# Hash attention and a SwiGLU layer in one kernel: earlier loads, and unit 1's x turned by DMA instead of TensorE

## The chip, the cores and the metric

The kernel runs on one core of a Trainium2 chip. The metric is the device time of one execution in microseconds (us). It is given as the median of several runs of the same program; 327.43 us is the median of three for the kernel before (327.17 to 328.53).

A core has five engines that run their own instruction streams: TensorE (PE, matmuls, with weight loads PEld beside them), VectorE (DVE), ScalarE (ACT), GpSimd (POOL) and SyncE (SP). SP computes nothing here; it issues DMAs, one after the other in the order written, and where a DMA must wait for something, all DMAs behind it on SP wait too. Sixteen DMA engines carry the data.

## The reference

```python
# attention: 4 batches, 8 heads, 768 rows, head size 64
q_bits = einsum('bhsd,dk->bhsk', q, proj) > 0        # 6 bits for each row; the same for k
mask   = bucket(q_bits)[..., :, None] == bucket(k_bits)[..., None, :]
scores = where(mask, q @ k.T / 8, -1e9)
attn   = exp(scores - max) / (sum + 1e-9)
x      = (attn @ v), heads side by side              # 3072 rows of 512
# feed-forward: 512 -> 1536 -> 512
xn  = x / sqrt(mean(x*x) + 1e-6) * rms_g
g   = xn @ w_gate
out = (g * sigmoid(g) * (xn @ w_val)) @ w_out
```

## The kernel before

The work is cut into eight **units**: unit u is half of batch u // 2, that is 384 query rows. In a unit there are eight heads, and a head is three **slots** of 256 keys each, so that attention is 192 slots, counted from 0. Heads of a batch go in four **pairs**; the text writes (1, 2) for batch 1, pair 2 (pairs count from 0, so it is the third pair of that batch). A pair's data are needed first by the unit of the batch's first half: pair (1, 2) by slot 60, in unit 2.

In slot t TensorE first computes the scores of slot t + 1 (`scores`, L345), ScalarE takes the exponential of slot t (`probs`, L357), and then whatever stands in `plan[t]` is recorded, in the order in which it was put there by `at(0, t, ...)`. There is no scheduler: each engine does its part of this list in that order, and waits where a semaphore tells it to. So the slot numbers in the code set the order on every engine, SP's DMA queue included, though not the time at which a DMA is issued: SP may run ahead of or behind the slots.

What the change touches, step by step:

- **Loads of a pair.** `load_natural` (L97) and `load_v` (L106) load q, k and v of a pair, 384 KB each, in three DMAs. From pair (1, 2) on `load_blocks` (L120) loads q and k instead in eight DMAs of 96 KB whose rows are 32 numbers (128 bytes) long. All go to a ring of eight buffers (`lpool`); a load waits until the last reader of its buffer is done.
- **Bits.** A pair's rows are multiplied by the projection on PE (`hash_pairs` L236 or `hash_one` L216), VectorE reads the signs (L225), and small DMAs carry these rows of bits into QK, the operand of the scores (`send_pair` L275, `send_bits` L304). A head's scores wait for its bits. `SENDS` gives the slot of such a send where it isn't that of the hash.
- **The turning of q and k** is done by PE for the pairs up to (1, 1) (L156) and by VectorE from (1, 2) on (`turn_dve`, L188 and L195); GpSimd then casts them into QK (`cast_pool`, L208).
- **v.** `v_prep` (L313) and `v_sum` (L319 to L321) are four GpSimd instructions for each pair. `zero_rows` (L146) is a GpSimd memset of one of six QK buffers.
- **x.** When a unit's heads are done, `norm` (L448, L456) scales its x, three thirds of 128 rows, and each third has to be turned, so that its 512 columns lie on the partitions. `turn_x` does that with four PE transposes into PSUM (L463) and one DVE multiplication by the column of weights `gcol` on the way out (L469, or L467 on ScalarE). `turn_dma` (L427) does it with one DMA transpose on SP's queue; the weights must then have been multiplied in before, along the row, and `norm` does that with `grow` (L448), a 128-row copy of `rms_g` that a DMA spreads and ScalarE multiplies by sqrt(512). `ONDMA` says how many of a unit's thirds go by DMA: two of three in units 2 to 6, one in unit 7, none in units 0 and 1.
- **The feed-forward part.** `gate` and `value` (L480) need all three thirds of the turned x (`xnT`). `project` (L509) and `store` (L521, L522) finish the unit before. `spread` places these pieces over the slots of the next unit: for unit 1 over slots 48 to 71. `norm(1)` stands in slot 52.
- **Weights.** Six `load_w` DMAs on GpSimd's queue (L581), 768 KB each, at slots 22 to 42, in the order wg, wv, wg, wv, wo, wo.

The table that places the pairs from (1, 2) on holds for each the slot of its loads, those of the turning of k and q, and that of the hash.

Of the kernel before, what the change touches and what calls it, by code (L numbers as in the profile page):

```python
# [19 lines left out]
DMODEL = H * D  # L20
# [13 lines left out]
def kernel(  # L34
# [12 lines left out]
    nc = tc.nc  # L47
# [27 lines left out]
    grow = const.tile([128, DMODEL], FP32, name="grow")  # L75
# [343 lines left out]

    rstds = {}  # L420

    ONDMA = {2: 2, 3: 2, 4: 2, 5: 2, 6: 2, 7: 1}

    def turn_dma(u, c):
        if c == 0:
# [16 lines left out]
    def norm(u):  # L442
# [3 lines left out]
        for c in range(3 if 0 < u < 7 else 2):  # L446
            if c < ONDMA.get(u, 0):
                nc.vector.scalar_tensor_tensor(  # L448
# [145 lines left out]
    def at(w, s, f, *a):  # L594
        plan[NS * w + s].append(lambda: f(*a))
# [70 lines left out]
    at(0, 1, load_natural, nc.sync, 0, 3, "q")  # L666
    at(0, 2, load_v, nc.sync, 0, 2)
    at(0, 2, load_v, nc.sync, 0, 3)
    at(0, 60, nc.sync.dma_start, grow, moe_rms_g.partition_broadcast(128))
    at(0, 65, nc.scalar.mul, grow, grow, float(DMODEL) ** 0.5)  # L670
    at(0, 6, v_prep, 0, 1)
    at(0, 15, v_prep, 0, 2)
    at(0, 19, v_prep, 0, 3, nc.vector)
# [6 lines left out]
        at(0, 39 + 3 * i, load_w, wo, moe_w_out, 6 * i, 6)  # L680


    for hp, ts in ((0, (8, 22, 23, 24, 25, 24, 39, 26, 28, 42)), (1, (20, 27, 28, 29, 30, 29, 41, 32, 33, 43))):
        tl, ts = ts[0], ts[1:]
        for w in "kq":
            at(0, tl, load_natural, nc.sync, 1, hp, w)
        at(0, tl, load_v, nc.sync, 1, hp)
        at(0, ts[0], new_pair, 1, hp)
        for t, hh, w in zip(ts[0:4], (0, 1, 0, 1), "kkqq"):
            at(0, t, turn_pe, 1, hp, hh, w)  # L690
        at(0, ts[4], cast_pool, 1, hp, "k")
        at(0, ts[5], cast_pool, 1, hp, "q")
        if hp == 0:
            at(0, ts[6], hash_pair, 1, hp)
            at(0, ts[7], send_pair, 1, hp)
        at(0, ts[8], v_prep, 1, hp)
        at(0, ts[8], v_sum, 1, hp)

    spots = {
# [10 lines left out]
    }  # L710
    for i, t in ((0, 39), (1, 41), (2, 57), (3, 61)):
        at(0, t, zero_rows, i)
    TX = 37

# [16 lines left out]
    for n, (u, h) in enumerate(order):  # L731
        t = 3 * n + 4 - ((u, h) == (0, H - 1))
# [46 lines left out]
            inserts[2 * b * NS + s] = (MEAN, v_mean, b, hp, 4)  # L779


    SENDS = {(2, 0, 0): 77, (2, 0, 1): 77, (2, 2, 1): 101, (3, 2, 1): 149}

    def place(t, step):
        at(0, t, *step)
        if step[0] is hash_one:
            late.append((t, hash_bits, *step[1:]))
            for hh in range(2):
                s = SENDS.get((*step[1:], hh), t)
                late.append((max(s, t), send_bits, *step[1:], hh))  # L790
# [26 lines left out]
    for u in range(7):  # L817
# [9 lines left out]
        at(0, t0 + 4, norm, u)  # L827
        for c in range(ONDMA.get(u, 0)):
            at(0, t0 + 5, turn_dma, u, c)
        pieces = []  # L830
        for i in range(9):
# [5 lines left out]
            if i in (6, 7):  # L837
                thirds = ((0,), (1, 2))[i - 6]
                for c in thirds:
                    if c >= ONDMA.get(u, 0):  # L840
                        pieces.append((TURN, False, [(0, turn_x, u, c)]))
# [10 lines left out]
    def behind_norm(t):  # L852

        return t - t % NS + 9 if 1 <= t % NS < 9 else t

    for (b, hp), (load, kturns, qturns, _) in spots.items():
        at(0, load, load_blocks, nc.sync, b, hp)
        at(0, load, load_v, nc.sync, b, hp)
        at(0, min(kturns + qturns), new_pair, b, hp)
        for w, turns in (("k", kturns), ("q", qturns)):  # L860
            for i, t in enumerate(turns):
                at(0, t, turn_dve, b, hp, w, i, len(turns))
            t = turns[-1] + 1
            at(0, t if (b, hp) == (1, 2) else behind_norm(t), cast_pool, b, hp, w)
        t = 54 if (b, hp) == (1, 2) else behind_norm(qturns[-1] + 2)
        at(0, t, v_prep, b, hp)
        at(0, t, v_sum, b, hp)

# [66 lines left out]
```

## Time and profile before

| | |
|---|---|
| median of three runs | 327.43 us (327.17 to 328.53) |
| the profiled execution | 327.66 us |
| its span, first to last instruction | 325.9 us (1.8 us lie around it) |
| PE busy | 321.1 us, 99% of the span |
| DVE, ACT, POOL busy | 231.0, 228.6, 157.6 us |
| granted TensorE clock | full in all 40 slices |
| moved by DMA | 32.6 MB, 100 GB/s on average, in 85,741 packets |

Times in the text are us from the span's start. "Busy" of PE is modelled: matmuls are pipelined, and what counts is the distance from the start of one to the start of the next. A row of the timeline gives the start, the length, engine, line, operation, tiles and the number of instructions merged into it; its length includes the latency of the last one.

By the starts of its scores on PE, slot 24 begins at 29.8 us, slot 48 at 62.8, slot 60 at 83.0 and slot 66 at 92.5.

### The profile page before, as it was taken

Reading aid. Unit: us, or ns where it says so; the run is one execution under the profiler, and the core shown is the slowest. Engines: PE = TensorE matmul, PEld = TensorE weight load, DVE = VectorE, ACT = ScalarE, POOL = GpSimd, SP = SyncE. Lnnn points to the kernel's source line nnn. Section 1 sums busy time; section 2 is a strip of 40 time slices with the busy share of each in tenths; the row PEclk is TensorE's granted clock in tenths of the full one; section 3 lists DMA queues with packets and bytes.
Section 4 is the critical chain, followed back from the end, with each engine's and each line's share of the span. In section 5 each row is a group of like instructions: output and inputs, shape, how many; then the busy total and the mean of one; then the engine's idle time right before and its main releaser. Section 6 shows DMA issues by size and latency. Waiting matters only on the chain.

```text
span 325.9 us, 7789 instructions
## 1 busy us (share of the span) xinstructions
PE 321.1 (99%) x2954; PEld 194.6 (60%) x2955; DVE 231.0 (71%) x514; ACT 228.6 (70%) x333; POOL 157.6 (48%) x204
## 2 busy tenths in 40 slices
PE   9999999999999999999999999999999999999996
PEld 4576666656566565655566556655656556665554
DVE  5887876869878659875888558886677536673870
ACT  6999887666688667777767668776777768754322
POOL 3999749955974353732783522753592111221000
PEclk9999999999999999999999999999999999999999
DMA  7942999989328828253547047002200030003002
GB/s 227 348 159 65 229 216 208 178 120 183 115 41 157 158 61 170 49 105 99 82 107 145 7 139 138 7 1 58 80 4 3 1 99 32 2 2 101 14 2 97
DMA packets 85741, 32.63 MB, mean 100 GB/s; under 512 B 70908, under 2 KB 82632, under 8 KB 85704
## 3 DMA queue, kind: packets, MB, share of 16 engines
q1 hardware_dynamic: 81800, 27.35, 35.9%
q0 software_dynamic: 3680, 4.72, 8.7%
q8 instruction: 23, 0.38, 0.5%
q14 instruction: 14, 0.11, 0.1%
q10 hardware_dynamic: 224, 0.07, 0.1%
HBM read 28.58 MB, written 6.29 MB: 107 GB/s over the span
## 4 chain that ended last, share of the span: by engine, by line
PE 98%; ACT 1%; issue 0%
PE s_ps L345 20%; PE g_ps L480 19%; PE v_ps L480 19%; PE y_ps L509 18%; PE o_ps L370 11%; PE d_ps L216 2%; PE t_ps L156 2%; PE d_ps L236 2%; PE z_ps L576 1%; PE x_ps L463 1%; PE y_ps L528 1%; PE m_ps L329 1%; ACT psb L357 1%; PE s_ps L156 0%; ACT ypart L533 0%
## 5 line engine op out<-in xcount | busy, mean ns | idle before, releaser
L357 ACT ACTIVATE psb<-s_ps,ebias 128x768 f16<-128x768 f32 x192 | 167.9, 900 | 21.3 <-PE s_ps L345 20.4
L345 PE MATMUL s_ps<-QK 128*128 128x384 f16 (+1 forms) x384 | 93.5, 326 | 1.2 <-ACT psb L357 1.1
L488 ACT ACTIVATE t<-g_ps 128x384 f32<-128x384 f32 x96 | 47.2, 492 | 51.1 <-PE g_ps L480 49.4
L480 PE MATMUL g_ps<-xnT,wg 128*128 128x384 f16 x384 | 82.7, 326 | 0.0
L480 PE MATMUL v_ps<-xnT,wv 128*128 128x384 f16 x384 | 81.8, 326 | 0.0
L497 DVE SCALAR_TENSOR_TENSOR a<-t,g_ps 128x384 f32<-128x384 f32 x96 | 52.9, 551 | 27.1 <-ACT t L488 25.4
L391 POOL TENSOR_TENSOR x<-otmp,rcp 128x384 f32<-128x384 f32 x30 | 25.1, 838 | 97.1 <-DVE rcp L389 96.9
L509 PE MATMUL y_ps<-wo,ht 128*128 128x512 f16 x276 | 67.7, 379 | 0.0
L498 DVE SCALAR_TENSOR_TENSOR ht<-a,v_ps 128x384 f16<-128x384 f32 x96 | 53.2, 554 | 12.0 <-PE v_ps L480 4.1
L370 PEld LDWEIGHTS <-psb 128*128 128x128 f16 x1152 | 51.9, 97 | 15.7 <-issue 1.2
L370 PE MATMUL o_ps<-vl,psb 128*128 128x65 f16 x1152 | 55.8, 193 | 0.0
L345 PEld LDWEIGHTS <-QK 128*128 128x128 f16 (+1 forms) x384 | 34.7, 98 | 34.9 <-issue 9.2
L480 PEld LDWEIGHTS <-wg 128*128 128x128 f16 x384 | 35.2, 97 | 21.2
L480 PEld LDWEIGHTS <-wv 128*128 128x128 f16 x384 | 35.1, 97 | 20.8 <-issue 0.2
L509 PEld LDWEIGHTS <-ht 128*128 128x128 f16 x276 | 24.9, 98 | 23.0
L521 ACT COPY ysb<-y_ps 128x512 f32<-128x512 f32 x23 | 13.5, 587 | 16.0 <-PE y_ps L509 16.0
L384 DVE TENSOR_TENSOR otmp<-o_ps,cvb 128x390 f32<-128x390 f32 x32 | 17.8, 558 | 7.2 <-PE o_ps L370 7.2
L208 POOL CAST QK<-qT 64x768 f16<-64x768 f32 x20 | 16.5, 823 | 10.4 <-DVE qT L195 9.5
L397 POOL TENSOR_TENSOR sq<-x 128x384 f32<-128x384 f32 x24 | 19.9, 827 | 1.9
L208 POOL CAST QK<-kT 64x768 f16<-64x768 f32 x20 | 16.4, 822 | 4.7 <-DVE kT L195 2.7
L469 DVE TENSOR_TENSOR xnT<-x_ps,gcol 128x512 f16<-128x512 f16 x11 | 7.4, 688 | 15.0 <-PE x_ps L463 14.9
L195 DVE STREAM_TRANSPOSE kT<-kL 128x192 f32<-128x192 f32 x32 | 16.4, 518 | 0.0
(85 smaller groups left out, 277.3 us busy)
## 6 DMA issues: line engine op xcount, KB each, us to landing
vn<-in_v_dram SPq DMA_DIRECT2D x16, 384.0 KB
out_dram<-ysb SPq DMA_DIRECT2D x23, 256.0 KB
qL<-in_q_dram SPq DMA_DIRECT2D x40, 96.0 KB
kL<-in_k_dram SPq DMA_DIRECT2D x40, 96.0 KB
kn<-in_k_dram SPq DMA_DIRECT2D x5, 384.0 KB
qn<-in_q_dram SPq DMA_DIRECT2D x5, 384.0 KB
wg<-in_moe_w_gate_dram POOLq DMA_DIRECT2D x2, 768.0 KB, 9.9
wv<-in_moe_w_val_dram POOLq DMA_DIRECT2D x2, 768.0 KB, 12.1
```

Source lines behind the costliest of these rows:

```text
L208: nc.gpsimd.tensor_copy(QK[b, 2 * hp + hh, "h"][0:64, o : o + S], src[64 * hh : 64 * hh + 64, :])
L345: nc.tensor.matmul(ps[:, j, 0:HALF], QK[b, h, "h"][rows, S + jt * 128 : S + (jt + 1) * 128], QK[b, h, "h"][rows, half * HALF : (half + 1) ...
L357: nc.scalar.activation(psb[u, h][:, 2 * ch : 2 * ch + 2, :], sps.pop((u, i))[:, :, 0:HALF], AF.Exp, bias=ebias, scale=ESCALE,)
L370: nc.tensor.matmul(o[:, c, hh, 0:65], psb[u, h][:, jt, c * 128 : (c + 1) * 128], vls[b % 2][:, h, 2 * (jt % 3) + jt // 3 if b in PARITY el ...
L384: nc.vector.tensor_add(tmp[:, :, :, 0:65], o[:, :, :, 0:65], cvb[b % 2][:, 2 * hp : 2 * hp + 2, 0:65].unsqueeze(1).to_broadcast([128, 3, 2 ...
L391: eng.tensor_mul(xd.rearrange("p c (h d) -> p c h d", h=2), tmp[:, :, :, 0:64], r.to_broadcast([128, 3, 2, 64]),)
L397: eng.tensor_mul(sq, xd, xd)
L480: nc.tensor.matmul(ps, w[:, kt, fs], xnT[u][:, kt, :], start=(kt == 0), stop=(kt == 3))
L488: nc.scalar.activation(t, fbank[u, ft, "g_ps"], AF.Tanh, scale=0.5)
L497: nc.vector.scalar_tensor_tensor(out=a, in0=t, scalar=1.0, in1=g, op0=ALU.add, op1=ALU.mult)
L498: nc.vector.scalar_tensor_tensor(out=ht[u][:, ft, :], in0=a, scalar=0.5, in1=vv, op0=ALU.mult, op1=ALU.mult)
L509: nc.tensor.matmul(y, ht[u][:, ft, c * 128 : (c + 1) * 128], wo[:, ft, :], start=(ft == 0), stop=(ft == NF - 1),)
```

## The change

Unit 1's first two thirds of x go by DMA instead of PE, and for that `grow` comes earlier: its load moves from slot 60 to 40, its multiplication on ScalarE from slot 65 to 49. Loads move: pair (1, 1) from slot 20 to 17, pair (1, 2) from 34 to 22, pair (2, 0) from 50 to 49. The bits of pair (1, 2), which is hashed in slot 51, are sent at slots 53 and 55, behind the DMA transposes. On GpSimd `v_prep` and `v_sum` of (1, 2) move from slot 54 to 57 and the memset of QK buffer 3 from slot 61 to 69. `spread` still leaves the two pieces of time where the PE transposes stood, so no other PE instruction changes its place.

```diff
-    ONDMA = {2: 2, 3: 2, 4: 2, 5: 2, 6: 2, 7: 1}
+    ONDMA = {1: 2, 2: 2, 3: 2, 4: 2, 5: 2, 6: 2, 7: 1}
...
-    at(0, 60, nc.sync.dma_start, grow, moe_rms_g.partition_broadcast(128))
-    at(0, 65, nc.scalar.mul, grow, grow, float(DMODEL) ** 0.5)
+    at(0, 40, nc.sync.dma_start, grow, moe_rms_g.partition_broadcast(128))
+    at(0, 49, nc.scalar.mul, grow, grow, float(DMODEL) ** 0.5)
...
-    for hp, ts in ((0, (8, 22, ..., 42)), (1, (20, 27, 28, 29, 30, 29, 41, 32, 33, 43))):
+    for hp, ts in ((0, (8, 22, ..., 42)), (1, (17, 27, 28, 29, 30, 29, 41, 32, 33, 43))):
...
-        (1, 2): (34, (48, 48), (46, 46), 51),
+        (1, 2): (22, (48, 48), (46, 46), 51),
         (1, 3): (45, (55, 56), (57, 58), 61),
-        (2, 0): (50, (63, 64, 65, 66), (67, 69, 70, 71), 73),
+        (2, 0): (49, (63, 64, 65, 66), (67, 69, 70, 71), 73),
...
-    for i, t in ((0, 39), (1, 41), (2, 57), (3, 61)):
+    for i, t in ((0, 39), (1, 41), (2, 57), (3, 69)):
         at(0, t, zero_rows, i)
...
-    SENDS = {(2, 0, 0): 77, (2, 0, 1): 77, (2, 2, 1): 101, (3, 2, 1): 149}
+    SENDS = {(1, 2, 0): 53, (1, 2, 1): 55, (2, 0, 0): 77, (2, 0, 1): 77, (2, 2, 1): 101, (3, 2, 1): 149}
...
-        t = 54 if (b, hp) == (1, 2) else behind_norm(qturns[-1] + 2)
+        t = 57 if (b, hp) == (1, 2) else behind_norm(qturns[-1] + 2)
         at(0, t, v_prep, b, hp)
         at(0, t, v_sum, b, hp)
```

More of the change, by code (lines that the diff above doesn't have):

```diff
@@ L680 @@
         at(0, 39 + 3 * i, load_w, wo, moe_w_out, 6 * i, 6)
-    for hp, ts in ((0, (8, 22, 23, 24, 25, 24, 39, 26, 28, 42)), (1, (20, 27, 28, 29, 30, 29, 41, 32, 33, 43))):
+    for hp, ts in ((0, (8, 22, 23, 24, 25, 24, 39, 26, 28, 42)), (1, (17, 27, 28, 29, 30, 29, 41, 32, 33, 43))):
         tl, ts = ts[0], ts[1:]
```

## The prediction

> **What bounds the kernel now.** I read the page first: the busy shares, then the chain that ended last.
>
> ```profile
> PE 321.1 (99%) x2954; PEld 194.6 (60%) x2955; DVE 231.0 (71%) x514; ACT 228.6 (70%) x333; POOL 157.6 (48%) x204
> ...
> PE 98%; ACT 1%; issue 0%
> ```
>
> TensorE is the bound from end to end, at the full granted clock, so PE instructions taken away are gain, and everything else counts only where it makes PE wait. How much waiting is left? Adding up start-to-start distances of the PE timeline against the usual step of each kind (a 384-column matmul 163 ns, a 512-column one 215 ns), the idle time left between 10 us and the end is about 4 us, in pieces under 0.6 us; from 60 to 90 us, where the change works, it is 0.6. So a gain over 0.5% (1.64 us) can hardly exist here; 0.5% is about what a measurement of this kernel can tell from no change.
>
> Second, the PE timeline where the removed instructions stand:
>
> ```profile
> 75.56 0.39 PE L463 MATMUL x_ps<-ident,xn 128*128 128x128 f16 x4
> 75.79 1.03 PE L509 MATMUL y_ps<-wo,ht 128*128 128x512 f16 x4
> ...
> 77.25 0.75 PE L463 MATMUL x_ps<-ident,xn 128*128 128x128 f16 x8
> 77.83 0.49 PE L345 MATMUL s_ps<-QK 128*128 128x384 f16 x2
> ...
> 79.30 0.49 PE L480 MATMUL g_ps<-xnT,wg 128*128 128x384 f16 x2
> ```
>
> From start to next start the first four transposes hold PE 0.23 us (56 ns each), the other eight 0.58 us. The first gate matmul, which needs all three thirds, starts at 79.30.
>
> Third, SP's timeline. This is where DMA transposes have to fit in:
>
> ```profile
> 61.93 5.31 SPq L120 DMA_DIRECT2D qL<-in_q_dram  x4
> 67.34 3.55 SPq L120 DMA_DIRECT2D kL<-in_k_dram  x4
> 71.40 0.39 SPq L106 DMA_DIRECT2D vn<-in_v_dram  x1
> 71.91 0.39 SPq L522 DMA_DIRECT2D out_dram<-ysb  x1
> 72.40 3.73 SPq L120 DMA_DIRECT2D qL<-in_q_dram  x4
> 76.23 2.66 SPq L120 DMA_DIRECT2D kL<-in_k_dram  x4
> 78.99 0.58 SPq L106 DMA_DIRECT2D vn<-in_v_dram  x1
> 79.67 5.73 SPq L304 DMA_DIRECT2D QK<-bits  x8
> ```
>
> In the kernel before, SP is still issuing loads of (1, 3) and (2, 0) until 79.57: no transpose could start at 75 us. Whether the earlier loads clear this is what decides.
>
> **PE, the gain.** Eight of twelve transposes go. The first group is worth 0.23. Of the second, four remain; in unit 4 four take 0.22 (190.54 to 190.76), so 0.58 - 0.22 = 0.36 goes (0.22 for four, the rest a wait on PSUM). Sum: 0.59 us. DVE loses two evictions of 0.69 (L469) and pays two scalings of 0.75 (L448) for two of 0.48 (L456); it isn't on the path.
>
> **When the DMA thirds are ready.** norm(1) starts on DVE at 73.86, set by `rstd`; the first scaled third ends 0.75 later. In unit 2 the same step goes from DVE 111.09 to SP's first transpose at 111.90, 0.81 us, so here SP could issue at 74.67. Unit 4 gives the tightest gate:
>
> ```profile
> 189.03 2.56 SPq L427 DMA_TRANSPOSE xnT<-xn  x2
> ```
>
> ```profile
> 192.22 0.49 PE L345 MATMUL s_ps<-QK 128*128 128x384 f16 x2
> 192.55 0.44 PE L370 MATMUL o_ps<-vl,psb 128*128 128x65 f16 x9
> 192.96 0.81 PE L480 MATMUL g_ps<-xnT,wg 128*128 128x384 f16 x4
> ```
>
> 3.93 us after the first issue the gate runs, with at most 0.14 us of wait before it (nine small matmuls take 0.27, and 0.41 lies between). So ready is at 74.67 + 3.9 = 78.6, and the gate now comes at 79.30 - 0.59 = 78.71. It just fits. Bounds: a wait of 0 to 0.3; I take 0.
>
> A sentence apart: the Trainium skill (VectorE: DVE Perf Modes, "The three transpose paths" and "Rules for kernel authors") says to transpose 128x128 on TensorE if PSUM may be the destination, and gives 390 ns there against 1309 ns by DMA. By that figure, my estimate for eight such blocks one after the other is 10.5 us, and the gate would wait some 6 us; the trace speaks against the sum, since in unit 2 the data of one instruction (four blocks) moves within 0.65 us, and both are through 3.4 us after the first issue.
>
> **SP and the DMA engines before 74.67.** DMA counts by the microsecond show the law that matters:
>
> ```profile
> q0 software_dynamic: 132, 0.20, 109.8%
> q1 hardware_dynamic: 133, 0.02, 21.5%
> ```
>
> ```profile
> q1 hardware_dynamic: 1054, 0.13, 84.5%
> ```
>
> The first two are 48 to 49 us: while a weight load runs (q0), SP's short block packets (q1) go one for one with it, 132 in a us. The third is 69 to 70 us: alone they go at about 1050. A pair has 6144 of them. In the kernel before, the loads of (1, 2) begin at 37.74, amid the weights, and SP needs until 58.7. After the change they begin at 29.6, after the bits of (0, 3), and move from about 30.9 (the lag in later loads is 1.3). The weights flow fully from 34.9, or, by the lag of the last one (issued 57.12, full at 60.0), from 33.6. So 2800 to 4200 packets pass freely and the rest with v go at 132, faster in the gaps at 42 to 44 and 51: through at 49 to 54. By SP's order each DMA waits for the one eight places before it, so the bits of (1, 1), `grow` and then (1, 3) come at 49 to 55; the last weights leave a free stretch at 56 to 60, and hold SP to 174 a us until 64.2. Left then are (2, 0) and at most half of (1, 3): 6 to 10 us. (2, 0) is through at 70.4 to 74.5, SP free a little sooner. The transposes' data would move 1.35 after issue, at 76.0: a margin of 1.5 us at the worst end.
>
> **What the early loads might hurt.** *Bits of (0, 3)* (wanted by slot 24, 29.82): they now queue behind (1, 1), three loads issued at 24.3. The load of (1, 0) took 4.6 us from first issue (17.61) to last data (22.2), so the rings are clear at 28.9; the bits' data moved at 28.0 to 29.0 anyway. Cost 0 to 0.3, I take 0. *Weights*: wv landed at 44.3 (33.41 + 10.9), wanted at 45.46. Beside block packets q0 kept its 130 a us (125 to 142 from 44 to 51, 118 to 140 alone), so 0; bound: what is left of a block load, 2.8 us of DMA time, less the 1.16 of slack, 1.6. *`grow`* lands before 60, ScalarE wants it at 66.6; its 0.64 us move within ACT's idle time. *Bits of (1, 2)*, now behind two transposes on SP: sent at 77.3 to 80.0 instead of 79.7 to 82.4, wanted at 83.0. Today slot 60 waits 0.14 us there; that may go, too. *GpSimd*: `v_prep` and `v_sum` of (1, 2) (2.9 us) leave a stretch where POOL idles afterwards (76.9 to 80.5) for one where it is full; the casts of (1, 3) move from 85.0 to 87.3, their first head is done at 89.9, its scores start at 91.9. The memset (2.65) fits later into an idle 3.4 us before 105.5. Leaving also frees DVE: one of norm(1)'s scalings took 1.22 instead of 0.48 beside these POOL instructions. All taken at 0; apart from the bits of (0, 3) each has about 1 us of cover or more.
>
> **Sum.** Span 325.9 - 0.59 = 325.3; the execution 327.66 - 0.6 = 327.1. This execution lies 0.23 over the median, so 327.43 - 0.6 = 326.8.
>
> **Rivals.**
> A, *slower: SP is not clear in time.* If the loads gain nothing, SP comes to the transposes at 79.6 as its timeline stands, ready is 83.5, and the gate waits 4.8: net +4.2, 331.6. Every us that SP is later than 74.8 costs one; from 75.4 on the change loses, from 77.0 it loses over 0.5%. For it: the packets beside the weights are slow, and a small error in where the weights begin moves thousands of them. Against: the free stretch at 56 to 60 absorbs both ends of that. The skill (TensorE: Matmul & The Clock Gate, Part 1) adds that an idle window of about 3.4 us halves PE's clock, which would add to so long a wait; no run here shows it. 0.16.
> B, *the gate waits for the DMA thirds although SP is clear*, by as much as was saved: 3.9 is an upper bound from a unit with an empty queue; a store and end of (2, 0) beside it may make 4.5. Then the change trades 0.6 for 0.5 and does nothing: 327.4 (327.1 to 327.9). This is how the skill's rule on transposes would come true, in small. 0.15.
> C, *the weights or the bits of (0, 3) come late* by half of their bounds or more: net +0.2 to +1.1, 327.6 to 328.5. 0.07.
> D, *more goes than the transposes*: waits elsewhere close up for over 1.6 us. There is hardly that much idle time. 0.04.
>
> **Numbers.** The forecast (326.3 to 327.1) has 0.58; with B and C the range to 328.6 holds 0.80. Within 0.5%: 0.58 + 0.15 + 0.07 = 0.80; slower 0.16 (A); faster 0.04 (D). The low end takes in both small waits and the scatter of the three runs (0.26 below the median).
>
> **What would show it.** Right: two transposes on SP starting at 74.6 to 74.9, four x_ps matmuls before the gate, the gate at 78.6 to 78.9 with no gap before it, and from there each stage 0.6 sooner. Load of (2, 0) issued by 73. Wrong: a transpose that starts after 75.4, or a PE gap before the gate (A, B), at slot 24 or at the first v_ps (C).

## The result, and the profile after

The changed kernel takes 330.56 us, the median of 15 executions, against 327.70 us for 15 of the kernel before: the ratio is 1.0095, with a 95% interval of 1.0079 to 1.0111. So it is slower by about 1%, some 3 us, where 326.8 us and no measurable change was forecast. The ratio leaves out two slow executions, among them the profiled one (670.76 us, its matmuls starting twice as far apart as usual), so the lines below come from another run of the changed kernel, named after_again. Its profiled execution took 330.52 us with a span of 328.6; the kernel before had 327.66 and 325.9.

The page of the changed kernel (after_again), the busy shares and the chain that ended last:

```profile
PE 321.2 (98%) x2946; PEld 194.2 (59%) x2947; DVE 228.6 (70%) x512; ACT 228.2 (69%) x333; POOL 156.9 (48%) x204
...
PE 96%; DVE 1%; DMA 1%; ACT 0%; issue 0%; SPq 0%; DVEq 0%
```

Eight matmuls fewer, as intended, and DMA now has 1% of a chain in which it did not figure before. The list of waits of the same run names where:

```profile
PEld L480 <- DMA xnT<-xn: 1.9, 1, 1.9
PEld L345 <- DMA QK<-bits: 0.9, 1, 0.9
```

The columns are the total, the number of times and the longest. The first wait is that of the gate for the DMA-turned thirds, the second one is at scores that wait for bits. The kernel before has no wait of PE for either DMA in this list. On the PE timeline of after_again:

```profile
30.04 0.44 PE L370 MATMUL o_ps<-vl,psb 128*128 128x65 f16 x9
31.32 0.48 PE L345 MATMUL s_ps<-QK 70*128 70x384 f16 x2 [0.84 <-DMA QK<-bits]
...
79.35 1.02 PE L509 MATMUL y_ps<-wo,ht 128*128 128x512 f16 x4
81.78 0.48 PE L480 MATMUL g_ps<-xnT,wg 128*128 128x384 f16 x2 [1.41 <-DVE kT L188]
```

Nine small matmuls take 0.27 us from start to start, so the scores of slot 24 could have come at 30.31 and came at 31.32: 1.01 us. Four 512-column matmuls take 0.86, so the gate could have come at 80.21 and came at 81.78: 1.57 us. (The releaser printed there, DVE, is no cause: the gate does not read kT. The list of waits names the DMA.)

Third, SP's timeline of after_again:

```profile
27.25 2.84 SPq L275 DMA_DIRECT2D QK<-bits  x4
...
48.31 8.18 SPq L275 DMA_DIRECT2D QK<-bits  x8
...
57.09 3.09 SPq L120 DMA_DIRECT2D qL<-in_q_dram  x4
...
69.11 3.65 SPq L120 DMA_DIRECT2D qL<-in_q_dram  x4
...
76.82 2.73 SPq L427 DMA_TRANSPOSE xnT<-xn  x2
```

The loads of (1, 2) go behind the bits of (0, 3), at 30.20, as planned, but (1, 3) begins at 57.09, (2, 0) at 69.11, and the transposes at 76.82. The scaling of x began at 75.36 on DVE (1.5 later than before, through a later start and the wait at slot 24), so with the 0.81 us of the forecast they were due at 76.17: SP was 0.65 us late.

One thing more differs, at the very end. The last instruction that computes is the same copy on ScalarE, first in the kernel before, then in after_again:

```profile
323.12 0.27 ACT L533 COPY ypart<-y_ps 128x128 f32<-128x128 f32 x1 [0.97 <-PE y_ps L528]
```

```profile
325.52 0.27 ACT L533 COPY ypart<-y_ps 128x128 f32<-128x128 f32 x1 [0.97 <-PE y_ps L528]
```

From its start to the end of the span it takes 2.75 us before and 3.13 us here. All 13 profiles with unit 1's transposes on DMA have 3.12 to 3.15, and the three without (before, and loads_only and loads_v11 below) 2.75 to 2.76: an end that is 0.38 us longer goes with the two transposes. SP's closing semaphore instructions (L930) begin with the copy before (323.2) and 1.2 us after its start here (326.7); why was not tested.

The account: the first scores start 0.54 later (7.86 against 7.32 before; in four executions of the changed kernel this start lies between 6.87 and 7.86, so it is scatter); slot 24 costs 1.01; the gate 1.57; the end 0.38; the transposes bring back 0.59, and after the gate 0.13. That is +2.78, and the span grew by 2.77 (325.88 to 328.65). The distance from unit 0's first gate (46.31) to unit 1's (81.78) is 35.47 against 34.49 before, 1.57 - 0.59 more, and to unit 2's (119.56) it is 37.78 against 37.91.

### The profile page after: what moved, and what is told of

The parts are those of the page before. It is cut to its first block, busy times and chain, and to the rows that moved or that the text cites. A ratio compares the mean times of both kernels' runs of the same rounds, so it can differ in the third digit from the quotient of the medians.

```text
span 668.9 us, 7782 instructions
## 1 busy us (share of the span) xinstructions
PE 664.7 (99%) x2947; PEld 311.9 (47%) x2947; DVE 233.5 (35%) x512; ACT 233.0 (35%) x333; POOL 157.4 (24%) x204
## 4 chain that ended last, share of the span: by engine, by line
PE 99%; POOL 1%; issue 0%; ACT 0%
PE v_ps L480 20%; PE g_ps L480 20%; PE s_ps L345 20%; PE y_ps L509 19%; PE o_ps L370 10%; PE d_ps L216 2%; PE t_ps L156 2%; PE d_ps L236 1%; PE z_ps L576 1%; PE y_ps L528 1%; PE x_ps L463 1%; PE m_ps L329 1%; POOL QK L178 0%; PE s_ps L156 0%; POOL vadd L319 0%
## 5 line engine op out<-in xcount | busy, mean ns | idle before, releaser
L345 PE MATMUL s_ps<-QK 128*128 128x384 f16 (+1 forms) x384 | 172.9, 558 | 0.3 <-POOL vadd L320 0.3
L480 PE MATMUL g_ps<-xnT,wg 128*128 128x384 f16 x384 | 159.6, 562 | 0.0
L480 PE MATMUL v_ps<-xnT,wv 128*128 128x384 f16 x384 | 159.1, 563 | 0.0
L509 PE MATMUL y_ps<-wo,ht 128*128 128x512 f16 x276 | 138.4, 681 | 0.0
L370 PEld LDWEIGHTS <-psb 128*128 128x128 f16 x1152 | 91.9, 132 | 47.8 <-issue 45.2
L370 PE MATMUL o_ps<-vl,psb 128*128 128x65 f16 x1152 | 96.8, 254 | 0.0
L345 PEld LDWEIGHTS <-QK 128*128 128x128 f16 (+1 forms) x384 | 53.1, 145 | 86.2 <-issue 77.3
L480 PEld LDWEIGHTS <-wg 128*128 128x128 f16 x384 | 53.7, 146 | 63.7 <-issue 63.6
L480 PEld LDWEIGHTS <-wv 128*128 128x128 f16 x384 | 53.6, 146 | 63.0 <-issue 63.0
L509 PEld LDWEIGHTS <-ht 128*128 128x128 f16 x276 | 38.5, 147 | 62.9 <-issue 62.5
```

The lines of the kernel that those rows point to most:

```text
L345: nc.tensor.matmul(ps[:, j, 0:HALF], QK[b, h, "h"][rows, S + jt * 128 : S + (jt + 1) * 128], QK[b, h, "h"][rows, half * HALF : (half + 1) ...
L370: nc.tensor.matmul(o[:, c, hh, 0:65], psb[u, h][:, jt, c * 128 : (c + 1) * 128], vls[b % 2][:, h, 2 * (jt % 3) + jt // 3 if b in PARITY el ...
L480: nc.tensor.matmul(ps, w[:, kt, fs], xnT[u][:, kt, :], start=(kt == 0), stop=(kt == 3))
L509: nc.tensor.matmul(y, ht[u][:, ft, c * 128 : (c + 1) * 128], wo[:, ft, :], start=(ft == 0), stop=(ft == NF - 1),)
```

## The experiments

Theory after the result: SP is late (the forecast's rival A), and the bits of (0, 3) are late (rival C). The rivals to that: the transposes themselves are slow beside a load (B), or something else costs the 3 us.

### Round 1: which part costs what

**after_again** is the changed kernel once more, with nothing edited.

> The changed kernel as it is, for a profile at the normal clock. Its 15 runs lie 0.95% above before (about 3 us). Theory A (SP is not clear when the DMA transposes are due): the first transpose starts after 77 us and PE idles 2 to 4 us ahead of the first gate of unit 1. Theory C (the bits of pair (0, 3) or the weights come late, since loads stand ahead of them): PE idles 2 us or more near 30 us or near 45 us, and the transposes start at 75 us as forecast. Theory B (transposes slow though SP is clear): idle ahead of that gate, at most 0.6 us; it can't give 3 us.

330.52 us profiled, median 331.22, ratio 1.0119 (1.0076 to 1.0162). Shown above: both A and C in part, and B (see round 2).

**loads_only** leaves x on TensorE and keeps all earlier loads.

```diff
-    ONDMA = {1: 2, 2: 2, 3: 2, 4: 2, 5: 2, 6: 2, 7: 1}
+    ONDMA = {2: 2, 3: 2, 4: 2, 5: 2, 6: 2, 7: 1}
```

> The change without the DMA transposes of unit 1 (its x is turned by PE as before); all loads, sends and GpSimd moves as in the change. Theory A: the loss hangs on the transposes and is gone, so 327.1 to 327.8, like before. Theory C: the loss stays and the 0.59 us of PE transposes come back on top, so 330.5 to 331.5.

328.42 us, ratio 1.0030 (1.0019 to 1.0040). The PE timeline of loads_only:

```profile
31.19 0.48 PE L345 MATMUL s_ps<-QK 70*128 70x384 f16 x2 [0.75 <-DMA QK<-bits]
```

The matmuls before it started at 30.00. So the wait at slot 24 is there without the transposes (0.92 us), and it belongs to the loads. The time fits neither of the two theories alone (327.1 to 327.8, or 330.5 to 331.5). A run of round 2 shows whether it is their whole price.

**turn_only** is the kernel before with unit 1's x on DMA and `grow` sooner, without any earlier load (lines shortened).

```diff
-    ONDMA = {2: 2, 3: 2, 4: 2, 5: 2, 6: 2, 7: 1}
+    ONDMA = {1: 2, 2: 2, 3: 2, 4: 2, 5: 2, 6: 2, 7: 1}
-    at(0, 60, nc.sync.dma_start, grow, ...)
-    at(0, 65, nc.scalar.mul, grow, grow, ...)
+    at(0, 40, nc.sync.dma_start, grow, ...)
+    at(0, 49, nc.scalar.mul, grow, grow, ...)
```

> The kernel before with unit 1's two thirds turned by DMA and the row of weights loaded at slot 40 and scaled at slot 49; the pair loads stay late, the bits of (1, 2) stay ahead of the transposes. My working for a transpose behind the old load backlog gives a first transpose at about 80 to 86 us and +4 us or more: 331 to 336, by every theory. If it is near 327 the forecast's picture of SP was wrong.

340.55 us, ratio 1.0390 (1.0373 to 1.0407). SP's and PE's timelines of turn_only:

```profile
85.19 2.63 SPq L427 DMA_TRANSPOSE xnT<-xn  x2
```

```profile
89.18 0.80 PE L480 MATMUL g_ps<-xnT,wg 128*128 128x384 f16 x2 [10.11 <-DMA xnT<-xn]
```

The order on SP decides: the transposes stand behind the loads of (2, 0) and here the bits of (1, 2) too, and the gate waits 10.27 us. That is more than the 331 to 336 expected; PE's clock was at half from 82.80 to 93.04, which is taken up below. The change, with earlier loads and the bits sent behind, has the transposes at 76.82 instead of 85.19. Note also the 3.99 us from issue to gate, with nothing of the loads left in the DMA rings (where packets that are issued wait for an engine).

**pair11_late** is the change with the loads of (1, 1) where they were (lines shortened).

```diff
-    ... (1, (17, 27, 28, 29, 30, 29, 41, 32, 33, 43))):
+    ... (1, (20, 27, 28, 29, 30, 29, 41, 32, 33, 43))):
```

> The change with pair (1, 1) loaded at slot 20 again, so that the bits of (0, 3) are sent ahead of that load. If theory C is right by those bits: back to 326.8 to 327.2. If it is right by the weights, or theory A holds: still 329.5 to 331.

335.87 us, ratio 1.0253 (1.0229 to 1.0276). The wait at slot 24 is gone, but SP's timeline of pair11_late shows the loads of (1, 2) deeper among the weights, and PE's a new wait at slot 48:

```profile
42.73 14.23 SPq L120 DMA_DIRECT2D kL<-in_k_dram  x4
```

```profile
62.18 0.49 PE L480 MATMUL v_ps<-xnT,wv 128*128 128x384 f16 x2
64.28 0.48 PE L345 MATMUL s_ps<-QK 128*128 128x384 f16 x2 [1.61 <-POOL x L391]
```

Issuing q and k of (1, 2) now lasts from 30.89 to 56.96, where in after_again it lasts from 30.20 to 44.01. The bits of batch 1's first pair, issued behind them, miss slot 48 by 1.77 us (again the printed releaser is only the last event the profile links; the bits' packets come last), and the gate waits 3.71. A late start at 30 us is paid more than once. So this run, far over all that was expected of it, cannot say what the bits of (0, 3) cost; loads_v11 below does.

### Round 2: taking the two waits away

**v11_behind** sends only v of (1, 1), which is not urgent, behind the bits of (0, 3), so that 384 KB fewer lie ahead of them.

```diff
-        at(0, tl, load_v, nc.sync, 1, hp)
+        at(0, 23 if hp else tl, load_v, nc.sync, 1, hp)
```

> The change with v of pair (1, 1) loaded behind (1, 2) (slot 23) instead of ahead of the bits of (0, 3). Theory now: the 1.0 us wait ahead of slot 24's scores comes from these bits standing behind 1.15 MB of loads in the same rings; with 0.77 MB ahead the rings are clear 1 us sooner and the wait falls to 0 to 0.3. Rival: the bits are late for another reason (the eight-DMA limit of SP, or DVE), then the wait stays near 1.0. The gate's wait should not get smaller (1.5 to 3.5), since v's 256 packets only move into the weights' time. Total 329 to 331.

332.25 us, ratio 1.0131 (1.0118 to 1.0144). Its PE timeline has no wait at slot 24: the nine small matmuls start at 30.02 and the scores at 30.30. But the gate now waits 3.08 us (transposes at 76.80, gate at 81.33). The DMA side did not move, so PE, a microsecond earlier at slot 24, only arrived earlier at the gate and waited there. Behind this wait PE's clock was at half for 3.4 us (see "The clock" below), and the kernel got slower still.

**loads_v11** is the same edit in loads_only, without the transposes:

> The run loads_only (no transposes by DMA in unit 1) with v of (1, 1) behind (1, 2). If the wait of the bits of (0, 3) is the whole loss of loads_only, it is back at before: 327.4 to 327.8. If the early loads cost something else, it stays near 328.4.

327.72 us, ratio 1.0001 (0.9992 to 1.0010). So the wait at slot 24 was all that the loads cost, and 384 KB ahead of those bits were its cause: shown. With that wait gone the moves even gain a little without any transpose by DMA: from unit 0's gate to unit 1's it takes 34.35 (34.49 before) and to unit 2's 37.78 (37.91).

**pair20_behind** issues the load of (2, 0) after the transposes and the bits of (1, 2), all of which now go in slot 53 (lines shortened).

```diff
-        (2, 0): (49, (63, 64, 65, 66), (67, 69, 70, 71), 73),
+        (2, 0): (54, (63, 64, 65, 66), (67, 69, 70, 71), 73),
-    SENDS = {(1, 2, 0): 53, (1, 2, 1): 55, ...}
+    SENDS = {(1, 2, 0): 53, (1, 2, 1): 53, ...}
```

> The change with the load of pair (2, 0) moved from ahead of the DMA transposes to behind them and behind the bits of (1, 2) (slot 54). Theory now: the gate's 1.5 us wait is SP's lateness by that load (0.65 us) plus its data still in the rings (about 1 us); the first transpose then starts 0.8 us after norm's scaling begins, the gate runs without a wait over 0.2, and only the 1.0 at slot 24 is left: 327.5 - 0.6 + 1.0 = 327.9. Rival (DMA transposes are slow by themselves): the gate still waits 0.5 or more, 328.5 to 329.5.

332.92 us, ratio 1.0143 (1.0121 to 1.0164). The gate waits no more: transposes 75.92, gate 80.00, 4.08 us apart. A wait of 2.72 us appears at slot 66 instead, and 0.66 us of the wait at slot 24 remain. The run **both** (v11_behind and pair20_behind in one kernel) shows it alone.

> The two together: no wait at slot 24, none at unit 1's gate, 0.6 us of PE transposes gone: 326.9 (0.2% under before). If both causes are right but something else in the early loads costs time, it shows here: 327.5 or more.

331.19 us, ratio 1.0101 (1.0079 to 1.0124). The PE and SP timelines of both:

```profile
78.74 0.49 PE L480 MATMUL g_ps<-xnT,wg 128*128 128x384 f16 x2
...
94.30 0.80 PE L345 MATMUL s_ps<-QK 128*128 128x384 f16 x2 [2.41 <-POOL x L391]
```

```profile
74.66 2.63 SPq L427 DMA_TRANSPOSE xnT<-xn  x2
...
90.96 5.99 SPq L304 DMA_DIRECT2D QK<-bits  x8
```

Here the forecast's own figures come true: transposes at 74.66 (74.67 forecast), the gate at 78.74 (78.71 forecast) with no gap before it. (That they agree so closely is partly luck, since the start of an execution scatters by a microsecond.) And yet the kernel is no better, since the bits of (1, 3), which slot 66 wants, stand behind the load of (2, 0), issued from 83.72, and go at 90.96. The matmuls before those scores started at 91.39 and take 0.33, the rest is the wait. Against v11_behind only the place of (2, 0) and the slot of one send of bits were changed: a wait of 3.08 at the gate became one of 2.58 at slot 66.

**turn_pair20_behind** asks whether the earlier loads are needed at all once (2, 0) is out of the way: turn_only with the lines of pair20_behind.

> The kernel before with unit 1's two thirds turned by DMA, the row of weights at slots 40 and 49, the bits of (1, 2) and then the load of (2, 0) behind the transposes; the loads of (1, 1) and (1, 2) stay where they were. If the place of (2, 0) on SP is all that the transposes need, no load has to be earlier: SP is free at 72.3, the gate doesn't wait, 326.9. If the transposes need the earlier loads of (1, 1) and (1, 2), the gate waits 1 us or more: 328 or above.

332.70 us, ratio 1.0151 (1.0118 to 1.0184). Transposes at 75.11, gate at 79.12 (4.01 later, a wait of 0.28), and 3.38 us of wait at slot 66. So they are hardly needed for the transposes; what lacks room is SP's queue after them.

### Round 3: the load of (2, 0) cut in two

**split** is both, with k of (2, 0) ahead of the transposes, and q and v behind the bits of (1, 2) (shown in short; `load_blocks` now takes the part to load).

```diff
+        at(0, 49, load_blocks, nc.sync, b, hp, "k")     # (2, 0) alone
+        at(0, 54, load_blocks, nc.sync, b, hp, "q")     # and v
```

> As the run of both, but the load of pair (2, 0) is cut: its k (four DMAs, 2.7 us of SP) ahead of the transposes at slot 49, where SP stood idle from 70.5 to 74.7, its q and v behind the bits of (1, 2) at slot 54. Theory: the 2.6 us wait at slot 66 in both came from the bits of (1, 3), sent at 91.0 because SP was still busy with (2, 0), though ready near 88.5; now SP is free at about 88, the bits go on time, no PE wait over 0.3 us is left after 30 us, and the 0.6 us of transposes show: 326.9. Rival (the transposes and the bits can't both be on time, whatever stands between them): a wait of 1 us or more at unit 1's gate or at slot 66, 328 or above.

327.91 us, ratio 1.0014 (1.0001 to 1.0027). The PE timeline of split (its lines are two further down than those of the kernel before):

```profile
45.39 0.81 PE L482 MATMUL g_ps<-xnT,wg 128*128 128x384 f16 x4
...
79.30 0.49 PE L482 MATMUL g_ps<-xnT,wg 128*128 128x384 f16 x2
```

No wait of PE over 0.2 us is left after 30 us. From gate to gate it takes 33.91 (34.49 before), and to unit 2's gate, at 117.08, 37.78 (37.91): 0.58 and 0.13 gained, the 0.59 and the 0.14 of the forecast. The time doesn't show it: this execution's first scores came 0.60 later than in the profile of before (7.92), and its end is 0.39 longer, as in every run with these transposes. The late start is scatter; the longer end is a cost, and leaves 0.3 of the 0.7.

**split_late_loads** cuts (2, 0) likewise, in turn_pair20_behind, with the loads at their old places:

> The same cut in the kernel before with late loads of (1, 1) and (1, 2) (the run turn_pair20_behind). SP is free there at 73.0 only: the four DMAs of k end at 75.7, 0.8 us late for the transposes, with up to 0.7 us of data still in the rings, so the gate waits 0.8 to 1.5 us, and slot 66 doesn't: 327.5 to 328.4. If it is 326.9 the early loads of (1, 1) and (1, 2) serve nothing at all.

329.16 us, ratio 1.0053 (1.0031 to 1.0074): transposes at 75.19, a wait of 0.34 at the gate and 0.59 at slot 66. The two waits are 0.93 together, and the median span is 0.95 longer than that of split (327.10 against 326.15); the rest of the difference between the two times lies outside the span. So the earlier loads, with the moves on GpSimd that this run leaves out too, are worth about 0.9 us here: with them every deadline is met.

### Round 4: does any margin remain, and what scatters?

**split_more** sends only two of the eight block DMAs of (2, 0) ahead of the transposes, and v behind the bits of (1, 3) (shown in short).

```diff
-        at(0, 49, load_blocks, nc.sync, b, hp, "k")
+        at(0, 49, load_blocks, nc.sync, b, hp, "k0")    # k of the first head
```

> The run split with less of (2, 0) ahead of the transposes: two DMAs of k there instead of four, the other two of k and the four of q behind the bits of (1, 2), v behind the bits of (1, 3) (slot 62). Theory: the runs of split scatter by 2.2 us because SP comes to the transposes with only 0.6 us in hand and the weights' start moves that; 1.4 us more in hand should close the scatter and let the gain of 0.6 be seen: 326.9 to 327.2, spread under 1.3 us. If the spread stays at 2 us the scatter comes from elsewhere.

328.17 us, ratio 1.0010 (1.0000 to 1.0020). Its profiled execution started early (first scores 6.95) and has a span of 325.1, 33.89 from gate to gate and no PE wait. That is the forecast kernel in its stages, and its own best execution; its median span is 326.0, the same as that of the kernel before beside it. Of the 0.7 us gained in the stages, the longer end takes 0.39; where the other 0.3 goes is open. That the median time is 0.3 over before although the spans are equal comes from the time around the span, 2.15 us here and 1.80 in before; no run shows why. The expectation missed twice: not 326.9 to 327.2, and a spread of 1.7 us instead of under 1.3, so SP's time in hand is not shown to be what scatters here.

**after_p2, after_p3 and after_p4** are three more profiled executions of the changed kernel, since its times spread from 328.6 to 334.0 (the kernel before: 327.2 to 328.5).

> The changed kernel once more, for another profile: its runs lie between 328.6 and 334. Theory: what varies is how many packets of (1, 2) pass ahead of the weights, and so when SP comes to the transposes; the gate's wait then follows the first transpose's start (start + about 4.5 to 5), and a wait over 3 us brings a lower granted clock behind it. The wait at slot 24 stays near 1.0. Rival: the wait at slot 24 varies as much, or the time is lost behind 100 us.

> The same kernel, a third profile; expected as for the second.

> The same kernel, a fourth profile; expected as for the second.

| | time, us | q of (1, 3) | transposes | gate | apart | wait at gate | to unit 2's gate | wait at slot 24 |
|---|---|---|---|---|---|---|---|---|
| after_again | 330.52 | 57.09 | 76.82 | 81.78 | 4.96 | 1.57 | 37.78 | 1.01 |
| after_p2 | 333.58 | 58.26 | 78.07 | 83.18 | 5.11 | 3.40 | 39.45 | 1.05 |
| after_p3 | 331.69 | 56.23 | 76.83 | 81.28 | 4.45 | 2.23 | 39.43 | 0.85 |
| after_p4 | 335.70 | 59.08 | 80.15 | 84.97 | 4.82 | 5.09 | 39.73 | 0.98 |

What scatters is the gate's wait, and behind it the time to unit 2's gate, 1.7 to 2.0 us longer in three of the four; that is the clock (see below). Slot 24's wait is about the same each time. On SP's timeline of after_p4 the q of (1, 3) was issued at 59.08 instead of 57.09 and so met the last weight load in full; it took 9.32 us where in after_again it took 3.09:

```profile
59.08 9.32 SPq L120 DMA_DIRECT2D qL<-in_q_dram  x4
```

Two microseconds there became 3.3 at the transposes. In the other three the transposes follow the start of (1, 3) too, except that the two earliest starts end alike (76.82 and 76.83).

## Why the prediction was wrong, by its steps

**The gain was right in size.** 0.59 for eight transposes (0.58 in split) and 0.14 at slot 60 (0.13). But loads_v11, in which PE still does all twelve transposes, has 0.14 of the first and all of the second: the wait on PSUM, which the forecast put down to the transposes, goes with the other moves. The transposes themselves are worth 0.44 (34.35 in loads_v11, 33.91 in split). That PE is the bound, that the weights, `grow` and GpSimd's work cost nothing: all borne out (loads_v11, 1.0001).

**Failed: nothing was priced for the end.** The forecast took 0.59 off the span and left the rest of it as it was. The end is 0.38 longer in every run with unit 1's transposes on DMA, which by itself takes back most of the 0.44.

**Failed: "2800 to 4200 packets pass freely".** In the DMA counts of after_again 31 to 32 us has 368 block packets. The next two microseconds:

```profile
q1 hardware_dynamic: 1011, 0.13, 81.1%
```

```profile
q0 software_dynamic: 26, 0.04, 88.8%
q1 hardware_dynamic: 189, 0.02, 15.1%
```

In 34 to 35 there are 117 and 45. That makes 1613 free packets. The data started in the second half of 31 and not at 30.9, and the weights' first packets came in 33, about the forecast's early end (33.6), after which the blocks fell at first to less than one for one. A window of 2.7 to 4.0 us at 1050 a us was reckoned as if the flow ran at full rate from end to end; only the count of 32 does. Yet this miss was half mended: in the gap between weight loads at 38 (942 packets) and 42 to 43 (814 and 532) the blocks caught up, and (1, 2) was through at about 53, inside the 49 to 54 that was forecast.

**Failed: "the bits of (1, 1), `grow` and then (1, 3) come at 49 to 55", and "the last weights leave a free stretch at 56 to 60".** The eight small DMAs of bits were issued from 48.31 to 56.49, each behind a load's place in the queue and beside weights that flowed until 57.7. (1, 3) began at 57.09; of the free stretch 195 and 997 packets at 58 and 59 us were left, and then the last weights came, issued 1.5 us later than before (58.61). So the blocks of (1, 3) took until 70 and those of (2, 0) until 77, not 70.4 to 74.5. That the free stretch "absorbs both ends of that" was wrong in kind: a stretch that is fixed by the weights helps only who arrives before it, so being late is made larger, not smaller (after_p4).

**Failed: ready 3.9 us after the first issue, at 78.6.** With empty rings it is nearly that: 3.99, 4.01 and 4.06 in turn_only, turn_pair20_behind and split_late_loads, where the gate waited for it, and at most 4.08 in pair20_behind and both, where the gate did not wait. Behind the data of (2, 0) it is 4.45 to 5.11 (the four executions of the changed kernel). Rival B named this with 4.5, and priced it at half a microsecond. In after_again B makes 1.06 of the wait and A 0.65, less 0.14 of slack, which gives the 1.57. That the data of (2, 0) are the cause of B is shown by pair20_behind, where they are gone and B with them.

**Failed: bits of (0, 3), "cost 0 to 0.3, I take 0".** Measured 0.85 to 1.05. The rings were indeed to be clear at 28.9; but the three loads were issued at 25.02, 25.51 and 26.25 (24.3 in the forecast), their packets ran at 222 to 257 a us until the end of 29, and the bits still had to land behind them. The time at which rings are clear was taken for the time at which data are there.

**Failed: three rivals that exclude each other.** A, B and C were given prices of which only A's made the kernel slower by over 0.5%. All three hang on one thing, that SP's queue and the DMA rings hold more between 25 and 95 us than the order leaves room for, so they came together: 0.65, 1.06 and 1.01, less the slack and the gain. Their sum was not priced.

**The clock.** Rival A noted that a long wait would be followed by half the clock, and that no run showed it. Now runs do. The windows of after_p3, by columns length, busy time of PE, PEld, DVE, ACT, POOL, granted clock, DMA share and GB/s:

```profile
82.00:83.00 1.00, 1.00 (x5) 0.47 (x4) 0.00 (x0) 0.36 (x1) 1.00 (x1) 0.55 0.02 5
83.00:84.00 1.00, 1.00 (x5) 0.46 (x4) 0.63 (x2) 0.92 (x2) 1.00 (x1) 0.50 0.47 183
84.00:85.00 1.00, 1.00 (x5) 0.50 (x4) 1.00 (x2) 0.00 (x0) 0.94 (x2) 0.50 0.24 89
85.00:86.00 1.00, 1.00 (x14) 0.81 (x13) 0.27 (x1) 0.00 (x0) 1.00 (x2) 0.75 0.04 9
```

The gate had waited 2.23 us, until 81.28; to 82 the clock was still 1.00, from there on it is about a half for 3.4 us. What is withheld from 82 to 86 sums to 0.45 + 0.5 + 0.5 + 0.25 = 1.7 us, three quarters of the wait itself. The Trainium skill (TensorE: Matmul & The Clock Gate, Part 1) puts the idle window that halves the clock at about 3.4 us; here a wait of 2.23 us was enough, and one of 1.57 (after_again) was not. Where the two differ the runs decide.

Length alone does not decide, though: turn_pair20_behind waited 3.38 us at slot 66, longer than after_p3, and kept its full clock. In the traces' clock half speed lasts 3.41 us (after_p2, after_p3, v11_behind, pair20_behind, both), 6.83 (pair11_late, after_p4) or 10.24 (turn_only), and the full speed before it 78.51 or 88.75, that is once, twice, three, 23 and 26 times 3.413. So the clock of these runs changes only in steps of 3.41 us. Stretches of such steps, two of after_p3 and two of turn_pair20_behind:

```profile
78.68:82.10 3.42, 1.36 (x9) 0.56 (x8) 1.90 (x4) 0.98 (x2) 1.94 (x3) 1.00 0.68 157
82.10:85.51 3.41, 3.41 (x20) 1.90 (x19) 1.90 (x3) 1.28 (x2) 3.35 (x3) 0.50 0.22 82
```

```profile
90.66:94.07 3.41, 1.60 (x18) 0.86 (x15) 1.80 (x4) 2.07 (x3) 3.27 (x3) 1.00 0.97 223
94.07:97.49 3.42, 2.01 (x20) 1.38 (x21) 1.00 (x3) 0.89 (x2) 1.07 (x2) 1.00 0.07 23
```

The whole wait of after_p3 lies in one stretch, in which PE is busy for 1.36 us, and the next one runs at half. The longer wait of turn_pair20_behind falls on two, with 1.60 and 2.01 us busy, and neither is followed by half speed. In all eight runs whose clock fell, PE was busy for at most 1.37 us in the stretch ahead of it. So what a wait costs depends on how it falls on these steps, which an edit can hardly steer. This was read from the runs there are and not tested by one of its own.

**What stays open**: why the end is 0.38 us longer with the two transposes, and where the other 0.3 us of the gain of split and split_more go. Also, why the last weight load starts 1.5 us later in after_again was not tried; the 0.54 of the start and the 1.01 at slot 24 add up to it.

## What to carry to other kernels

A move on a queue that is full can hand a wait to the next deadline on that queue instead of removing it: here slot 24, slot 48, the gate and slot 66 in turn. List every deadline behind a queue with its margin and add the lateness along the queue, instead of pricing each place as a separate case. A transfer with slack can be cut, so that only what must go first goes first; cutting one 1.1 MB load in two did what moves of whole loads could not, and even so won back only the loss.

## What was not expected of the hardware

- PE's clock went to half for 3.4 us after a wait of 2.23 us at full load around it, and stayed full after 1.57 us and, in another kernel, after 3.38 us that fell on two of the clock's steps: a wait can cost nearly twice its length, or not.
- Two DMA transposes of 128x512 have a time of 4.0 us from first issue to use that hardly varies when the rings are empty (3.99 to 4.06, three runs), and 0.4 to 1.1 us more behind a block load.
- The end of the program, far from the change, is 0.38 us longer in all 13 profiles with unit 1's two DMA transposes than in the three without.
- The short packets beside a weight load go one for one with it (133 to 133 in after_again at 48 to 49 us), but come fewer when a weight load begins: 45 against 117 and 98 against 129 in the two microseconds from 34. The Trainium skill (DMA: Bandwidth & Descriptors, Queues, rings and completion order) says that an engine takes its queues in turn, packet by packet; the steady counts agree, the first two microseconds do not. Why they differ is not shown: too few short packets may have been queued.
